# Attention scores as plain float32 matmuls on two halves of TensorE's rows, in place of a split into two fp32r parts

## The chip, the cores and the metric

One core of a Trainium2 chip runs the kernel. The metric is the device time of one execution in microseconds (us), median of several runs.

## The reference

Two stages. Attention with a learned relative position bias: batch 4, 8 heads, 576 positions, head dimension 64. Then a feed-forward stage with the maximum of three projections.

```
scores = q @ k.T / sqrt(64)                              # 4 x 8 x 576 x 576
x      = log1p(|i - j|) / log1p(max(i, 1))
bias   = relu(x * w1 + b1) @ w2                          # hidden 32, one bias per head
attn   = softmax(scores + bias);  attn /= sum(attn) + 1e-9
y      = attn @ v                                        # to 2304 x 512
h      = max(y @ w1m, y @ w2m, y @ w3m)                  # d_ff 768
out    = h @ w_out
```

Inputs of the attention are float32; the weights of the feed-forward stage are float64.

## The kernel before

**Bias stage.** 36 groups of 16 rows of the bias are computed (`hid` on VectorE and ScalarE, products `bp` on TensorE, scaled copies `bs`) and written to a DRAM tensor `bias_d` by DMA. SyncE (SP) issues all DMAs in program order. During this stage the first q and k are loaded and prepared (`prep(0)`, spread over groups 5 to 9), those of the second unit are loaded at group 16, and the first rows of the bias are read back (`load_bias`).

**Attention.** There are 16 units: 4 pairs of heads times 4 batches. For each unit `load_qk` brings q and k in twice, to partitions 0 to 63 and again to 64 to 127 (four DMAs). `prep` splits them: `qh` is q rounded to fp32r, `ql` the rest, `ks` holds k rounded on the lower partitions and its rest on the upper ones. It issues four casts and one subtraction on VectorE and three subtractions on GpSimd, one or two instructions after each of five steps. One matmul over 128 rows then gives q-part times (k high + k low), and two of them (`qh`, `ql`) make one half of a score tile.

A unit has 9 steps: for each of 4 tiles of 128 query rows one step for each of the two heads, and a last step for the 64 rows that are left of both heads (they stand together on 128 rows). In each engine the instructions run in program order, so the order in `step` is the schedule:

- `norm(n-2)`: VectorE adds 1e-9 and takes the reciprocal of the sums, GpSimd scales the exponentials `e` by it.
- `front(n)`: TensorE makes the scores of one head in `s` (two PSUM buffers), VectorE adds the bias and takes the minimum (`shift` below; a custom instruction and a read of its accumulator).
- `expo(n-1)`: ScalarE takes the exponential.
- `pvq`: up to two of the queued products of a group of query rows with v are run. A group has 5 entries in the queue: 4 pairs (each two matmuls of 64 output columns, one for each head, on the two halves of TensorE's columns) and one for the left-over keys (`vl`, all 128 columns), then a copy on ScalarE (`xhi`) and a subtraction on VectorE (`xlo`). The groups are 256 and 320 rows.
- `back(n-4)`: TensorE transposes `e` (four blocks into `tp`, and one or two into `lp`), ScalarE copies them to `et`; VectorE copies 1 to 3 of the 9.

A float32 matmul is recorded as two instructions (two passes), an fp32r one as one.

**Feed-forward stage.** It follows when the last `xhi` and `xlo` are there, and isn't touched by the change; the conversion of its first weights (`w0`) is done in small pieces between attention steps.

Of the kernel before, what the change touches and what calls it, by code (L numbers as in the profile page):

```python
# [19 lines left out]
def kernel(  # L20
# [12 lines left out]
    nc = tc.nc  # L33
# [131 lines left out]
    # attention, one pair of heads at a time  # L165
    units = [(hp, b) for hp in range(HP) for b in range(B)]
    order = [(t, h) for t in range(NTQ) for h in range(2)] + [(NTQ, 0)]
    NS = len(order)

    TS = 2  # L170
    sched = [(un, i) for un in range(len(units)) for i in range(NS)]
    NSTEP = len(sched)
    LAG = 4

    class Attention:
        def __init__(self, pool):
            self.pool = pool
            self.data = {}
            self.st = {}
            self.et = {}  # L180
            self.pvq = []
            self.preps = []
            self.vl = [pool.tile([128, 2 * D], F32, name=f"vl{x}", bufs=1) for x in range(2)]
            for x in self.vl:
                nc.gpsimd.memset(x, 0.0)
            bias_t.extend(pool.tile([128, 2, S], F32, name=f"bias{t}", bufs=1) for t in range(NTQ))
            bias_t.append(pool.tile([128, S], F32, name="biasm", bufs=1))

        def load_qk(self, un):
            pool, (hp, b) = self.pool, units[un]  # L190
            kr = pool.tile([128, 2 * S + 64], F32, tag="kr", bufs=1, name=f"kr{un}")
            qr = pool.tile([128, 2, S + 64], F32, tag="qr", bufs=1, name=f"qr{un}")
            hs = slice(2 * hp, 2 * hp + 2)
            for dst, src in ((kr, kd[b, hp]), (qr, qd[b, :, hs])):
                for x in (0, 64):
                    nc.sync.dma_start(out=dst[x:x + 64], in_=src)
            self.data[un] = dict(kr=kr, qr=qr)
# [12 lines left out]
        def prep(self, un):  # L210
            pool, u = self.pool, self.data[un]
            kr, qr = u.pop("kr"), u.pop("qr")
            ks = pool.tile([128, 2 * S + 64], F32R, tag="ks", bufs=2, name=f"ks{un}")
            qh = pool.tile([128, 2, S + 64], F32R, tag="qh", bufs=2, name=f"qh{un}")
            ql = pool.tile([128, 2, S + 64], F32R, tag="ql", bufs=2, name=f"ql{un}")
            u.update(ks=ks, qh=qh, ql=ql)
            p = slice(64, 128)
            kc = (slice(0, S), slice(S, 2 * S + 64))

            def sub_k(h):  # L220
                r = kc[h]
                nc.gpsimd.tensor_tensor(out=ks[p, r], in0=kr[p, r], in1=ks[p, r].bitcast(F32), op=ALU.subtract)  # L222

            def sub_q(h):
                nc.gpsimd.tensor_tensor(out=ql[:, h], in0=qr[:, h], in1=qh[:, h].bitcast(F32), op=ALU.subtract)

            nc.vector.tensor_copy(ks[:, kc[0]], kr[:, kc[0]])
            yield
            sub_k(0)
            nc.vector.tensor_copy(qh[:, 0], qr[:, 0])  # L230
            yield
            sub_q(0)
            nc.vector.tensor_copy(ks[:, kc[1]], kr[:, kc[1]])
            yield
            sub_k(1)
            nc.vector.tensor_copy(qh[:, 1], qr[:, 1])
            yield
            (nc.vector if un else nc.gpsimd).tensor_tensor(out=ql[:, 1], in0=qr[:, 1],
                                                           in1=qh[:, 1].bitcast(F32), op=ALU.subtract)
            yield  # L240

        def front(self, n):
            un, i = sched[n]
            t, h = order[i]
            pool, u = self.pool, self.data[un]
            s = ps_s(f"s{un}_{i}")
            ks, qh, ql = u["ks"], u["qh"], u["ql"]
            for x in range(2):
                r = slice(128 * t, 128 * t + 128)
                c0 = HALF * x  # L250
                ops = [(w, h, S * h + c0) for w in (qh, ql)]
                if t == NTQ:
                    ops += [(w, 1, S + LEFT + c0) for w in (qh, ql)]
                for j, (w, e, c) in enumerate(ops):
                    nc.tensor.matmul(s[:, x, 0:HALF], lhsT=w[:, e, r], rhs=ks[:, c:c + HALF],  # L255
                                     start=(j == 0), stop=(j == len(ops) - 1))
            sn = pool.tile([128, S], F32, tag="sn", bufs=2, name=f"sn{un}_{i}")
            nm = pool.tile([128, 1], F32, tag="nm", bufs=4, name=f"nm{un}_{i}")
            bt = bias_t[t][:, h] if t < NTQ else bias_t[t]
            nc.vector.tensor_tensor_reduce(  # L260
                out=sn.rearrange("p (a b) -> p a b", a=2), in0=s[:, :, 0:HALF],
                in1=bt.rearrange("p (a b) -> p a b", a=2), op0=ALU.add, op1=ALU.min,
                scale=-0.125, scalar=3e38, accum_out=nm)
            self.st[n] = (sn, nm)

        def expo(self, n):
            pool = self.pool
            sn, nm = self.st[n]
            h = order[sched[n][1]][1]
            if h == 0:  # L270
                self.e2 = pool.tile([128, 2 * S], F32, tag="e", bufs=3, name=f"e{n}")
            e = self.e2[:, S * h:S * h + S]
            sm = pool.tile([128, 1], F32, tag="sm", bufs=4, name=f"sm{n}")
            nc.scalar.activation(e, sn, ACTF.Exp, scale=-1.0, bias=nm, accum_out=sm)  # L274
            self.st[n] = (e, sm, self.e2)

        def norm(self, n):
            e, sm, e2 = self.st[n]
            rc = self.pool.tile([128, 1], F32, tag="rc", bufs=4, name=f"rc{n}")
            nc.vector.tensor_scalar(out=sm, in0=sm, scalar1=1e-9, scalar2=None, op0=ALU.add)  # L280
            nc.vector.reciprocal(rc, sm)  # L281
            nc.gpsimd.tensor_scalar(out=e, in0=e, scalar1=rc, scalar2=1.0, op0=ALU.mult, op1=ALU.mult)  # L282
            self.st[n] = (e, e2)

        def back(self, n):
            un, i = sched[n]
            t, h = order[i]
            pool, st = self.pool, self.st
            e, e2 = st.pop(n)
            ts = TS  # L290
            g = 0 if t < ts else 1
            w = 128 * ts if g == 0 else S - 128 * ts
            if i in (0, 2 * ts):
# [4 lines left out]
            c0 = 128 * t - 128 * ts * g  # L298
            tp = ps_t(f"tp{un}_{i}")
            for c in range(NTQ):  # L300
                k0 = 128 * c + LEFT * h
                nc.tensor.transpose(tp[:, 128 * c:128 * c + 128], e[:, k0:k0 + 128], ident)  # L302
            if t < NTQ:
                o, src = ea[:, :, h, c0:c0 + 128], tp.rearrange("p (c q) -> p c q", c=NTQ)
            else:
                o, src = ea[:, :, :, c0:c0 + LEFT], tp.rearrange("p (c h q) -> p c h q", c=NTQ, h=2)
            if i in ((4, 5, 6) if n < NSTEP - 102 else (5,)):
                nc.vector.tensor_copy(o, src)
            else:
                nc.scalar.copy(o, src)  # L310
            if t == NTQ or h == 1:
                lp = psum.tile([128, 128], F32, tag="l", bufs=1, name=f"lp{un}_{i}")
                m = 128 if t < NTQ else LEFT
                if t < NTQ:
                    nc.tensor.transpose(lp, e2[:, LB:S + LEFT], ident)
                else:
                    nc.tensor.transpose(lp, e[:, LB - 64:S], swap)
                    nc.tensor.transpose(lp[0:64], e[:, LB:S], ident)
                nc.scalar.copy(el[:, c0:c0 + m], lp[:, 0:m])
            if i == 2 * ts - 1 or i == NS - 1:  # L320
                self.queue_pv(un, 128 * ts * g, w, ea, el)
# [24 lines left out]
        def step(self, n, more=None):  # L346
            if 0 <= n - 2 < NSTEP:
                self.norm(n - 2)
            if n < NSTEP:
                un, i = sched[n]  # L350
                hp, b = units[un]
                nxt = un + 1
                if un < len(units) - 1:
                    if i == 0 and un:
                        self.load_qk(nxt)
                    if i == 8:
                        self.load_v(nxt)
                    if i == 3:
                        self.preps.append(self.prep(nxt))
                self.front(n)  # L360
                if b == B - 1 and hp + 1 < HP:
                    if i % 2 == 1 or i == NS - 1:
                        load_bias(hp + 1, i // 2)
            if more is not None:
                next(more, None)
            if 0 <= n - 1 < NSTEP:
                self.expo(n - 1)
            if len(self.pvq) == NTQ + 1 and self.wait:
                k, self.wait = 0, False
            else:  # L370
                k = 2 if len(self.pvq) >= 3 else 1
            if 0 <= n - LAG < NSTEP:
# [212 lines left out]
```

## Time and profile before

| | |
|---|---|
| median of 3 runs | 639.22 us (638.99 to 639.39) |
| profiled execution, span from the first instruction to the last | 637.4 us |
| bias stage, to the first `shift` | 0 to 61.2 us |
| attention, to the first matmul of the feed-forward stage | 61.2 to 338.2 us |
| feed-forward stage | 338.2 to 637.4 us |

Of the profiled execution only the span is recorded; the runs' median is 1.8 us above it, which is what lies around the span. Times in the rows below are us from the span's start, durations us; those in the groups of instructions are the total in us and the mean in ns. "[0.61 <-DVE nm L260]" is idle time of that engine ahead of the instruction, and what ended it. PE is TensorE's matmuls, PEld its weight loads, DVE VectorE, ACT ScalarE, POOL GpSimd, SP SyncE.

### The profile page before, as it was taken

What the parts mean: (1) busy time and instruction counts of PE and PEld (TensorE: products, weight loads), DVE (VectorE), ACT (ScalarE), POOL (GpSimd) and SP (SyncE); (2) the same over time, 40 slices, a digit from 0 to 9 for tenths busy, and PEclk for the clock granted to TensorE, in tenths of its full rate; (3) what the DMA queues carried; (4) which work ended last, traced back from release to release, by engine and by line L of the source; (5) the groups of instructions that cost most, each with busy time, mean ns of one, the idle gap of its engine ahead of it and who ended that gap; (6) DMA issues with size and microseconds to landing.
All of it is one profiled execution on the core that took longest, in us unless ns stands there. A gap on an engine that the chain in (4) does not pass through costs nothing.

```text
span 637.4 us, 11303 instructions
## 1 busy us (share of the span) xinstructions
PE 606.6 (95%) x3960; PEld 469.2 (74%) x3960; DVE 429.3 (67%) x1164; ACT 293.5 (46%) x747; POOL 199.0 (31%) x203
## 2 busy tenths in 40 slices
PE   7679899999998999989999999999999999999997
PEld 4224667767776777767777888888888888888886
DVE  7986989979997999889964564655655464123331
ACT  7668667767776877767781000000000001034443
POOL 1200777767775777777740000000000000000000
PEclk9998999999999999999999999999999999999999
DMA  8688643754467446763201122112212120001111
GB/s 214 191 256 288 172 118 92 208 142 99 100 195 191 98 100 167 187 143 92 63 2 34 34 66 67 58 42 67 67 34 82 51 67 0 1 34 67 67 66 67
DMA packets 48376, 65.12 MB, mean 102 GB/s; under 512 B 22464, under 2 KB 31936, under 8 KB 48320
## 3 DMA queue, kind: packets, MB, share of 16 engines
q1 hardware_dynamic: 48320, 64.40, 36.5%
q8 instruction: 32, 0.52, 0.4%
q14 instruction: 24, 0.20, 0.1%
HBM read 48.77 MB, written 15.61 MB: 101 GB/s over the span
## 4 chain that ended last, share of the span: by engine, by line
PE 58%; DVE 22%; DMA 6%; issue 4%; POOL 4%; ACT 3%; SPq 2%; DVEq 0%; POOLq 0%; ACTq 0%
PE h L464 8%; PE h L463 8%; PE h L462 8%; DVE sn L260 6%; PE g L464 4%; PE g L463 4%; PE g L462 4%; PE o L487 4%; PE o L488 4%; DMA qr<-in_qd_dram 4%; PE o L486 4%; PE pv L334 3%; PE tp L302 3%; DVE hid L106 3%; PE s L255 3%
## 5 line engine op out<-in xcount | busy, mean ns | idle before, releaser
L282 POOL TENSOR_SCALAR e<-e,rc 128x576 f32<-128x576 f32 x144 | 121.7, 848 | 116.8 <-DVE rc L281 82.4
L274 ACT ACTIVATE e<-sn,nm 128x576 f32<-128x576 f32 x144 | 113.1, 786 | 53.4 <-DVE nm L260 37.5
L469 ACT COPY m<-h 128x512 f32<-128x512 f32 (+1 forms) x30 | 16.4, 546 | 202.8 <-PE h L464 196.3
L255 PE MATMUL s<-ks,qh 128*128 128x288 f32 x320 | 101.4, 334 | 3.9 <-DVE nm L260 3.7
L302 PE MATMUL tp<-ident,e 128*128 128x128 f32 x576 | 90.2, 279 | 8.6 <-POOL e L282 8.2
L260 DVE CUSTOM_DVE_ANT_0 sn<-s,bias 128x576 f32<-128x576 f32 x128 | 96.1, 751 | 3.1 <-PE s L255 2.9
L302 PEld LDWEIGHTS tp<-ident,e 128*128 128x128 f32 x576 | 65.9, 140 | 42.9 <-POOL e L282 26.8
L255 PE MATMUL s<-ks,ql 128*128 128x288 f32 x320 | 89.0, 294 | 0.0
L462 PE MATMUL h<-xhi,wh 128*128 128x512 f32 (+1 forms) x240 | 88.6, 369 | 0.0
L463 PE MATMUL h<-xlo,wh 128*128 128x512 f32 (+1 forms) x240 | 88.3, 368 | 0.0
L464 PE MATMUL h<-xhi,wl 128*128 128x512 f32 (+1 forms) x240 | 88.3, 368 | 0.0
L310 ACT COPY et<-tp 128x512 f32<-128x512 f32 x119 | 70.0, 588 | 20.2 <-PE tp L302 19.9
L334 PE MATMUL pv<-et,vt 128*64 128x320 f32 (+1 forms) x512 | 76.0, 418 | 0.1
L255 PEld LDWEIGHTS s<-ks,qh 128*128 128x128 f32 x320 | 60.3, 188 | 6.8 <-DVE nm L260 6.0
L255 PEld LDWEIGHTS s<-ks,ql 128*128 128x128 f32 x320 | 60.6, 189 | 0.0
L127 PE MATMUL bp<-hid,w2s 128*32 128x79 f32 (+48 forms) x640 | 42.8, 404 | 12.0 <-DVE hid L106 7.2
L222 POOL TENSOR_TENSOR ks<-kr,ks 64x576 fp32r<-64x576 f32 (+1 forms) x32 | 49.2, 1536 | 14.7 <-DMA bias_d<-bs 11.1
L441 DVE TENSOR_TENSOR hl<-ht,hh 128x128 fp32r<-128x128 f32 x108 | 23.4, 287 | 44.9 <-ACT hh L440 44.9
L463 PEld LDWEIGHTS h<-xlo,wh 128*128 128x128 f32 x240 | 45.3, 189 | 7.6
L462 PEld LDWEIGHTS h<-xhi,wh 128*128 128x128 f32 x240 | 45.3, 189 | 7.6
L464 PEld LDWEIGHTS h<-xhi,wl 128*128 128x128 f32 x240 | 45.2, 188 | 7.5
L470 DVE TENSOR_TENSOR m<-h,m 128x512 f32<-128x512 f32 (+1 forms) x30 | 19.1, 637 | 46.8 <-ACT m L469 46.7
(77 smaller groups left out, 1032.5 us busy)
## 6 DMA issues: line engine op xcount, KB each, us to landing
bias_d<-bs SPq DMA_DIRECT2D x36, 295.5 KB, 4.3
qr<-in_qd_dram SPq DMA_DIRECT2D x32, 320.0 KB, 6.1
kr<-in_kd_dram SPq DMA_DIRECT2D x32, 304.0 KB, 4.5
bias<-bias_d SPq DMA_DIRECT2D x16, 576.0 KB, 4.0
w<-in_moe_w_dram SPq DMA_DIRECT2D x18, 512.0 KB, 3.5
out_dram<-ot SPq DMA_DIRECT2D x17, 256.0 KB, 2.0
vt<-in_v_dram SPq DMA_DIRECT2D x32, 128.0 KB, 2.4
w64o<-in_moe_w_out_dram SPq DMA_DIRECT2D x6, 512.0 KB, 3.6
```

Of the source, the lines that this page charges most:

```text
L127: nc.tensor.matmul(bp[32 * c:32 * c + 32, o:o + w], lhsT=w2s, rhs=src, start=True, stop=True)
L222: nc.gpsimd.tensor_tensor(out=ks[p, r], in0=kr[p, r], in1=ks[p, r].bitcast(F32), op=ALU.subtract)
L255: nc.tensor.matmul(s[:, x, 0:HALF], lhsT=w[:, e, r], rhs=ks[:, c:c + HALF], start=(j == 0), stop=(j == len(ops) - 1))
L260: nc.vector.tensor_tensor_reduce(out=sn.rearrange("p (a b) -> p a b", a=2), in0=s[:, :, 0:HALF], in1=bt.rearrange("p (a b) -> p a b", a=2) ...
L274: nc.scalar.activation(e, sn, ACTF.Exp, scale=-1.0, bias=nm, accum_out=sm)
L282: nc.gpsimd.tensor_scalar(out=e, in0=e, scalar1=rc, scalar2=1.0, op0=ALU.mult, op1=ALU.mult)
L302: nc.tensor.transpose(tp[:, 128 * c:128 * c + 128], e[:, k0:k0 + 128], ident)
L310: nc.scalar.copy(o, src)
L334: nc.tensor.matmul(pv[p], lhsT=u["vt"][:, c, h], rhs=ea[:, c, h], start=(c == 0), stop=False)
L462: nc.tensor.matmul(o, lhsT=hi[:, r], rhs=x, start=(c == 0), stop=False)
L463: nc.tensor.matmul(o, lhsT=hi[:, r], rhs=y, start=False, stop=False)
L464: nc.tensor.matmul(o, lhsT=lo[:, r], rhs=x, start=False, stop=(c == KDM - 1))
```

## The change

`prep` is gone, with its buffers. q and k stay float32 and are loaded once: head 0 of the pair on partitions 0 to 63, head 1 on 64 to 127, one DMA each (the host lays them out so). A step is now a tile of query rows of both heads, so a unit has 5 steps. Its scores are four float32 matmuls, two on the upper and two on the lower 64 rows of TensorE, each head into a PSUM buffer of its own; those of the left-over rows are two matmuls over all 128 rows, in which zeros in q keep the heads apart. The lag between `front` and the transposes goes from 4 steps of a head to 2 steps of a pair, sums are normalized for two heads at a time, VectorE always copies the transposes of head 1, and up to three entries of `pvq` run in a step, behind the transposes where they stood ahead of them.

```diff
-    LAG = 4
+    LAG = 2
         def load_qk(self, un):
-            kr = pool.tile([128, 2 * S + 64], F32, tag="kr", bufs=1, name=f"kr{un}")
-            qr = pool.tile([128, 2, S + 64], F32, tag="qr", bufs=1, name=f"qr{un}")
...
+            ks = pool.tile([128, S + LEFT], F32, tag="ks", bufs=2, name=f"ks{un}")
+            qs = pool.tile([128, S + LEFT], F32, tag="qs", bufs=2, name=f"qs{un}")
+            nc.sync.dma_start(out=qs, in_=qd[b, hp])
+            nc.sync.dma_start(out=ks, in_=kd[b, hp])
-        def prep(self, un):
...
         def front(self, n):
+            ss = [ps_s(f"s{un}_{t}_{h}") for h in range(nh)]
             for x in range(2):
+                for h in range(nh):
+                    if t < NTQ:
+                        p, r = slice(64 * h, 64 * h + 64), slice(128 * t, 128 * t + 128)
+                        c = LEFT * (1 - h) + HALF * x
+                    else:
+                        p, r, c = slice(0, 128), slice(LB, LB + 128), LEFT + HALF * x
+                    nc.tensor.matmul(ss[h][:, x, 0:HALF], lhsT=qs[p, r], rhs=ks[p, c:c + HALF],
+                                     start=True, stop=True)
...
         def step(self, n, more=None):
+            m, f = n - 1, n - LAG
...
+                    if t == 0 and un:
+                        self.load_qk(un + 1)
+                    if t == 4:
+                        self.load_v(un + 1)
+                nh = self.heads(n)
+                self.front(n)
+                self.shift(n, 0)
+            back = 0 <= f < NSTEP
+            if back:
+                tps, left = self.flip(f)
+                nc.scalar.copy(*tps[0])
+            if nh:
+                self.expo(n, 0)
+            if nh > 1:
+                self.shift(n, 1)
+            if n < NSTEP and b == B - 1 and hp + 1 < HP:
+                load_bias(hp + 1, t)
+            if 0 <= m < NSTEP:
+                self.norm(m)
+            if nh > 1:
+                self.expo(n, 1)
+            if back:
+                nc.scalar.copy(*left)
+                if len(tps) > 1:
+                    nc.vector.tensor_copy(*tps[1])
             if more is not None:
+                for _ in range(2):
+                    next(more, None)
+            k = 3 if len(self.pvq) >= 3 else 2
+            run, self.pvq = self.pvq[:k], self.pvq[k:]
+            for x in run:
+                x()
+            if back:
...
+                if t in (TS - 1, NS - 1):
+                    self.queue_pv(un, 128 * TS * g, w, *self.et)
@@ bias stage and attention loop
-                    first = at.prep(0)
-                if 5 <= g < 10:
-                    next(first)
-            at.step(n, w0 if n >= NSTEP - 102 and n % 3 == 0 else None)
+            at.step(n, w0 if n >= NSTEP - 57 and n % 3 == 0 else None)
```

`shift`, `norm` and `flip` hold the same instructions as `front`, `norm` and `back` did, for two heads at a time; `flip` issues the transposes of both heads and of `lp`.

## Rows read from the trace of the kernel before

**Rows 1.** The page of the profile: busy time by engine, and the chain of work that ended last by engine.

```profile
PE 606.6 (95%) x3960; PEld 469.2 (74%) x3960; DVE 429.3 (67%) x1164; ACT 293.5 (46%) x747; POOL 199.0 (31%) x203
...
PE 58%; DVE 22%; DMA 6%; issue 4%; POOL 4%; ACT 3%; SPq 2%; DVEq 0%; POOLq 0%; ACTq 0%
```

**Rows 2.** Busy time of each engine in the last two units (start:end, length, then busy time and number of instructions of each engine, granted clock, DMA share, GB/s).

```profile
297.85:314.92 17.07, 16.45 (x120) 12.43 (x118) 15.96 (x48) 12.90 (x33) 12.62 (x13) 1.00 0.45 107
314.92:329.59 14.67, 14.24 (x104) 11.25 (x105) 11.37 (x43) 11.89 (x31) 7.10 (x10) 1.00 0.06 21
```

**Rows 3.** Timeline of VectorE: the last `shift` of units 0, 3, 4 and 15.

```profile
74.44 0.76 DVE L260 CUSTOM_DVE_ANT_0 sn<-s,biasm 128x576 f32<-128x576 f32 x1
...
124.41 0.75 DVE L260 CUSTOM_DVE_ANT_0 sn<-s,biasm 128x576 f32<-128x576 f32 x1
...
143.36 0.76 DVE L260 CUSTOM_DVE_ANT_0 sn<-s,biasm 128x576 f32<-128x576 f32 x1
...
329.59 0.76 DVE L260 CUSTOM_DVE_ANT_0 sn<-s,biasm 128x576 f32<-128x576 f32 x1 [0.16 <-PE s L255]
```

**Rows 4.** Timeline of VectorE between the second and the third of these: a cast of `prep` that waits.

```profile
133.05 0.46 DVE L227 CAST ks<-kr 128x576 fp32r<-128x576 f32 x1 [1.60 <-DMA kr<-in_kd_dram]
```

**Rows 5.** Timeline of one and a half steps of unit 8: TensorE, its weight loads, and one row of VectorE.

```profile
200.36 0.60 PE L302 MATMUL tp<-ident,e 128*128 128x128 f32 x4
...
200.71 0.38 PE L255 MATMUL s<-ks,qh 128*128 128x288 f32 x1
...
200.93 0.30 PE L255 MATMUL s<-ks,ql 128*128 128x288 f32 x1
...
201.06 0.30 PE L255 MATMUL s<-ks,qh 128*128 128x288 f32 x1
...
201.20 0.29 PE L255 MATMUL s<-ks,ql 128*128 128x288 f32 x1
...
201.42 1.30 PE L334 MATMUL pv<-et,vt 128*64 128x320 f32 x8
...
202.65 0.66 PE L302 MATMUL tp<-ident,e 128*128 128x128 f32 x4
...
203.65 0.08 DVE L260 DVE_READ_ACCUMULATOR2_ANT nm<- 128x1 f32 x1
203.79 0.19 PEld L255 LDWEIGHTS s<-ks,qh 128*128 128x128 f32 x1 [0.61 <-DVE nm L260]
...
203.90 0.19 PEld L255 LDWEIGHTS s<-ks,ql 128*128 128x128 f32 x1
```

**Rows 6.** Timeline of TensorE: the left-over keys' matmul (two passes over 320 columns), behind a score matmul, and, in the end phase, behind a pair.

```profile
207.48 0.70 PE L331 MATMUL pv<-et,vl 128*128 128x320 f32 x2
...
337.81 0.81 PE L331 MATMUL pv<-et,vl 128*128 128x320 f32 x2
```

**Rows 7.** Groups of instructions on line 334: number of records, and their shortest, median and longest duration in ns.

```profile
L334 PE MATMUL pv<-et,vt x512: 379/432/484, 72.9 to 337.4; 128*64 128x256 f32 x86, 128*64 128x320 f32 x85
```

**Rows 8.** Groups of instructions on TensorE in the last unit, 314.92 to 329.59 us.

```profile
L334 PE MATMUL pv<-et,vt 128*64 128x320 f32 x16 | 2.6, 445 | 0.0
...
L334 PE MATMUL pv<-et,vt 128*64 128x256 f32 x8 | 1.1, 392 | 0.0
```

**Rows 9.** Timeline: a score's last matmul and the `shift` that waited for it; then VectorE's sequence of a `shift`, the two instructions of `norm` and the next `shift`.

```profile
324.76 0.29 PE L255 MATMUL s<-ks,ql 128*128 128x288 f32 x1
...
325.09 0.76 DVE L260 CUSTOM_DVE_ANT_0 sn<-s,bias 128x576 f32<-128x576 f32 x1 [0.46 <-PE s L255]
...
63.18 0.76 DVE L260 CUSTOM_DVE_ANT_0 sn<-s,bias 128x576 f32<-128x576 f32 x1
...
63.90 0.15 DVE L280 TENSOR_SCALAR sm<-sm 128x1 f32<-128x1 f32 x1
64.09 0.16 DVE L281 RECIPROCAL rc<-sm 128x1 f32<-128x1 f32 x1
64.17 0.74 DVE L260 CUSTOM_DVE_ANT_0 sn<-s,bias 128x576 f32<-128x576 f32 x1
```

**Rows 10.** Groups of instructions of the whole trace: GpSimd's scaling, ScalarE's exponential, VectorE's copy of a transpose.

```profile
L282 POOL TENSOR_SCALAR e<-e,rc 128x576 f32<-128x576 f32 x144 | 121.7, 848 | 116.8 <-DVE rc L281 82.4 <-ACT e L274 17.9 <-PE tp L302 5.9
L274 ACT ACTIVATE e<-sn,nm 128x576 f32<-128x576 f32 x144 | 113.1, 786 | 53.4 <-DVE nm L260 37.5 <-DVE sm L280 15.5
...
L308 DVE COPY et<-tp 128x512 f32<-128x512 f32 x25 | 17.1, 682 | 0.9 <-PE tp L302 0.9
```

**Rows 11.** Timeline of VectorE in the bias stage, around the casts of `prep(0)` (a row of several instructions runs from the first one's start to the last one's end).

```profile
12.52 0.46 DVE L227 CAST ks<-kr 128x576 fp32r<-128x576 f32 x1
12.88 2.39 DVE L106 TENSOR_SCALAR hid<-sm,bp 128x480 f32<-128x480 f32 x3
...
21.18 6.44 DVE L106 TENSOR_SCALAR hid<-sm,bp 128x432 f32<-128x432 f32 x15
```

**Rows 12.** Timeline of SP in the bias stage: the load of the second unit's q and k.

```profile
32.21 1.33 SPq L196 DMA_DIRECT2D kr<-in_kd_dram  x2
33.64 1.23 SPq L196 DMA_DIRECT2D qr<-in_qd_dram  x2
```

**Rows 13.** The chain of work that ended last, in order of time, at that place.

```profile
34.96 7.38 DMA bias_d<-bs
```

**Rows 14.** Timeline of SP: the read of the left-over rows' bias, after the bias stage.

```profile
70.61 0.48 SPq L161 DMA_DIRECT2D biasm<-bias_d  x1
```

More of the change, by code (lines that the diff above doesn't have):

```diff
@@ L166 @@
     units = [(hp, b) for hp in range(HP) for b in range(B)]
-    order = [(t, h) for t in range(NTQ) for h in range(2)] + [(NTQ, 0)]
-    NS = len(order)
+    NS = NTQ + 1
     TS = 2
-    sched = [(un, i) for un in range(len(units)) for i in range(NS)]
+    sched = [(un, t) for un in range(len(units)) for t in range(NS)]
     NSTEP = len(sched)
-    LAG = 4
+    LAG = 2
     class Attention:
@@ L208, in load_v, with heads, front @@
             self.data[un].update(vt=vt, vl=vl)
-        def prep(self, un):
+        def heads(self, n):
+            return 2 if sched[n][1] < NTQ else 1
+        def front(self, n):
+            un, t = sched[n]
             pool, u = self.pool, self.data[un]
[L212 to L247, printed above, removed]
-            for x in range(2):
[L249 to L258, printed above, removed]
+            nh = self.heads(n)
@@ L259, in front, with shift @@
+            self.st[n] = dict(s=ss)
+        def shift(self, n, h):
+            un, t = sched[n]
+            pool, st = self.pool, self.st[n]
+            sn = pool.tile([128, S], F32, tag="sn", bufs=3, name=f"sn{n}_{h}")
+            nm = pool.tile([128, 1], F32, tag="nm", bufs=4, name=f"nm{n}_{h}")
             bt = bias_t[t][:, h] if t < NTQ else bias_t[t]
             nc.vector.tensor_tensor_reduce(
-                out=sn.rearrange("p (a b) -> p a b", a=2), in0=s[:, :, 0:HALF],
+                out=sn.rearrange("p (a b) -> p a b", a=2), in0=st["s"][h][:, :, 0:HALF],
@@ L262, in front @@
                 in1=bt.rearrange("p (a b) -> p a b", a=2), op0=ALU.add, op1=ALU.min,
                 scale=-0.125, scalar=3e38, accum_out=nm)
[L264 to L269, printed above, removed]
-            if h == 0:
[L271 to L275, printed above, removed]
+            st[h] = (sn, nm)
@@ L279, in norm @@
-            rc = self.pool.tile([128, 1], F32, tag="rc", bufs=4, name=f"rc{n}")
+            st, nh = self.st[n], self.heads(n)
+            sm = st["sm"][:, 0:nh]
+            rc = self.pool.tile([128, 2], F32, tag="rc", bufs=3, name=f"rc{n}")
             nc.vector.tensor_scalar(out=sm, in0=sm, scalar1=1e-9, scalar2=None, op0=ALU.add)
-            nc.vector.reciprocal(rc, sm)
-            nc.gpsimd.tensor_scalar(out=e, in0=e, scalar1=rc, scalar2=1.0, op0=ALU.mult, op1=ALU.mult)
-            self.st[n] = (e, e2)
@@ L285, in back @@
[L285 to L293, printed above, removed]
+            nc.vector.reciprocal(rc[:, 0:nh], sm)
+            for h in range(nh):
+                e = st["e"][:, S * h:S * h + S]
+                nc.gpsimd.tensor_scalar(out=e, in0=e, scalar1=rc[:, h:h + 1], scalar2=1.0,
+                                        op0=ALU.mult, op1=ALU.mult)
@@ L297, in back @@
             ea, el = self.et
[L298 to L302, printed above, removed]
+            c0 = 128 * t - 128 * TS * g
+            tps = []
+            for h in range(self.heads(n)):
+                tp = ps_t(f"tp{un}_{t}_{h}")
+                for c in range(NTQ):
+                    k0 = S * h + 128 * c + LEFT * h
+                    nc.tensor.transpose(tp[:, 128 * c:128 * c + 128], e2[:, k0:k0 + 128], ident)
+                if t < NTQ:
+                    o, src = ea[:, :, h, c0:c0 + 128], tp.rearrange("p (c q) -> p c q", c=NTQ)
+                else:
+                    o, src = ea[:, :, :, c0:c0 + LEFT], tp.rearrange("p (c h q) -> p c h q", c=NTQ, h=2)
+                tps.append((o, src))
+            lp = psum.tile([128, 128], F32, tag="l", bufs=1, name=f"lp{un}_{t}")
+            m = 128 if t < NTQ else LEFT
             if t < NTQ:
-                o, src = ea[:, :, h, c0:c0 + 128], tp.rearrange("p (c q) -> p c q", c=NTQ)
+                nc.tensor.transpose(lp, e2[:, LB:S + LEFT], ident)
             else:
[L306 to L321, printed above, removed]
+                nc.tensor.transpose(lp, e2[:, LB - 64:S], swap)
+                nc.tensor.transpose(lp[0:64], e2[:, LB:S], ident)
+            return tps, (el[:, c0:c0 + m], lp[:, 0:m])
         def queue_pv(self, un, c0, w, ea, el):
@@ L346, in step @@
         def step(self, n, more=None):
-            if 0 <= n - 2 < NSTEP:
-                self.norm(n - 2)
+            m, f = n - 1, n - LAG
+            nh = 0
             if n < NSTEP:
-                un, i = sched[n]
+                un, t = sched[n]
                 hp, b = units[un]
[L352 to L359, printed above, removed]
-                self.front(n)
-                if b == B - 1 and hp + 1 < HP:
-                    if i % 2 == 1 or i == NS - 1:
-                        load_bias(hp + 1, i // 2)
@@ L364, in step @@
-            if more is not None:
[L365 to L372, printed above, removed]
-                run, self.pvq = self.pvq[:k], self.pvq[k:]
-                for f in run:
-                    f()
-                self.back(n - LAG)
-            if self.preps:
-                for _ in self.preps[0]:
-                    break
-                else:
-                    self.preps.pop(0)
+                if un + 1 < len(units):
+                    if t == 0 and un:
+                        self.load_qk(un + 1)
+                    if t == 4:
+                        self.load_v(un + 1)
```

47 lines of the change are left out of this document (32 added, 15 removed).

## Prediction, before the change was run

> **What bounds the kernel now.** I read the page first: TensorE is busy 95% of the span and leads the chain of waits with 58%, VectorE follows with 22% [rows 1]. A busy TensorE is not yet a full one, since its matmuls overlap, so I then went to the attention's timeline and counted starts. The reader should look at distances between starts, not at durations. Four score matmuls of 288 columns start 0.13 us apart though each lasts 0.29 [rows 5]. Transposes: four end 0.60 after the first start, the last one lasting 0.27, so they start 0.109 apart [rows 5]. The left-over keys' two float32 passes over 320 columns take 0.70 with an end of 0.43, so one pass holds the engine 0.27 [rows 6]; that is 2 cycles a column at the granted clock of 1.00, the upper level of 2.4 GHz [rows 2]. Eight passes of the pairs take 1.30 together [rows 5], one lasting 0.43 [rows 7]: one behind the other they would need 7 x 0.27 + 0.43 = 2.3. So the two halves of the columns run side by side, and a pair costs 0.54 at 320 columns and 0.43 at 256.
>
> TensorE changes its shape around each burst of pairs. Without a change the pairs' first load would start at 201.20 + 0.13 = 201.33; it starts at 201.42, and the first load (0.05) lies open: 0.145. Back, the last pass ends at 201.42 + 1.30 - 0.43 + 0.27 = 202.56, the transposes' first load comes at 202.65 and is open for 0.06: 0.15 [rows 5].
>
> A unit then needs of TensorE: 40 score matmuls x 0.131 = 5.24; 42 transposes x 0.109 = 4.58; pairs and left-overs 5 x 0.54 + 5 x 0.43 = 4.85; four bursts of pairs with 4 x (0.145 + 0.15) = 1.18. Sum 15.85. The last unit tests it: it has no `prep` beside it, and lacks 8 of 32 passes of the pairs [rows 8], one burst: 15.85 - 0.86 - 0.30 = 14.69, against 14.67 measured [rows 2]. So without `prep` the old order is bound by TensorE. With it a unit takes (329.59 - 74.44) / 15 = 17.01 on the average, and 143.36 - 124.41 = 18.95 where a pair of heads begins [rows 3]; there VectorE's cast waits for q and k that come behind the bias loads [rows 4], and everything behind it on VectorE waits too. What `prep` costs is thus about 1.2 us a unit, and this is the most that its removal can give there.
>
> **The change, part by part.** *What goes.* VectorE's busy time falls from 15.96 to about the 11.37 of the unit without `prep`, GpSimd's from 12.6 to 7.1 [rows 2]; both are then far from a bound. Four loads of a unit become two.
>
> *Scores.* Four float32 matmuls of two passes, each 0.27 x 288/320 = 0.242. With the heads side by side 4 x 0.242 = 0.97 for a tile of both, against 8 x 0.131 = 1.05; the left-over tile 2 x 2 x 0.242 = 0.97. A unit: 4.84 in place of 5.24. No row shows matmuls on halves of the rows; the nearest, on halves of the columns, run fully side by side [rows 5, 7], and one behind the other would be 1.94. I take 0.97 and keep 1.94.
>
> TensorE also hides each load behind the pass before it in the same rows: 0.131 a matmul leaves no room for a 128-column load, of which 0.11 shows where it is open (203.79 to 203.90) [rows 5]. The Trainium skill (TensorE: Matmul & The Clock Gate, part 3, The mechanism) says that a load overlaps running matmuls only when its row group differs; by that three more loads of 0.11 would be open in each tile, 1.3 us a unit; these rows contradict it for the plain mode.
>
> *Changes of shape.* The new order is scores on row halves, transposes on the full array, pairs on column halves. Into row halves: 0.09 and an open load of 0.11 (as 203.79 to 203.90 [rows 5]), 0.20; four a unit, 0.79. From there to the transposes 0.15 x 4 = 0.60. Into the pairs 0.145 x 4 = 0.58. From pairs to `vl`, now in one step, 0.20 x 2 = 0.39 (0.81 for the two passes there against 0.70 shows the open load [rows 6]). Together 2.36, against 1.18. That row halves are changed into at the price of column halves is an estimate; the bounds are 0 and twice it. TensorE's need: 4.84 + 4.58 + 4.85 + 2.36 = 16.63, 0.8 more than before.
>
> *A new wait.* One step now takes both score buffers, so `front(n+1)` waits for both `shift`s of step n. From the first load: 0.11 + 0.97 to the last column; `shift` starts 0.33 behind the start of a 0.13 matmul [rows 9], so 0.20 behind the last column: at 1.28. The second follows 0.74 later, at 2.02, and lasts 0.76 (63.18 and 63.90 [rows 9]); a load that waited for one started 0.06 behind the read of its accumulator (203.73 to 203.79 [rows 5]): 2.85. A step with pairs holds TensorE 3.4 us or more and hides this. But a unit's ten queue entries run as 3 and 2, 3 and 2, so that one step in five (t = 1) has none; it has 0.11 + 0.97, 0.15, six transposes 0.65, done at 1.9. The next scores: head 0's first half runs while TensorE waits; the other three start at 2.85 and end at 2.85 + 0.11 + 0.97 = 3.93, where without the wait it would be 1.9 + 0.09 + 0.11 + 0.97 = 3.07. Lost: 0.86. `norm` of the step before stands on VectorE behind both `shift`s, at 2.74, and takes 0.35 (63.90, 64.09 and 0.16 [rows 9]); GpSimd scales two heads at 0.85 each [rows 10], until 4.8; the transposes of head 1 would start at 3.93 + 0.15 + 0.44 = 4.52: 0.28 more. The copy and subtraction of the product before lie ahead of the first `shift` on VectorE, behind two exponentials of 0.79 [rows 10] on ScalarE; I estimate 0.15. Sum 1.29, bounds 0.8 and 2. A unit: 16.63 + 1.29 = 17.92, 0.91 more than before; 15 units: +13.6.
>
> The other edits are hidden. `load_bias` of a tile is issued behind both its `shift`s and has five steps until it is read; what stands behind it on SP (`load_v`, `load_qk`) is needed a unit later. On the engines: VectorE has, for a tile, two `shift`s, `norm`, and a copy of 0.68 [rows 10], 0.74 x 2 + 0.35 + 0.68 = 2.5 of 3.4. The conversions of `w0` come two at a time from step 23 on; where they meet the step without pairs they delay it: +1 (0 to 3).
>
> *First unit and end.* From the first `shift` to the last one of unit 0 it is now 74.44 - 61.2 = 13.2; three waits of 2.9 and one of 2.3 make 11.1, but the left-over rows' bias is only asked for at 70.61, 9.4 behind the first `shift` [rows 14], and lands later: I take 12, -1. The end phase stays at 338.2 - 329.6 = 8.6: the transposes of two tiles and the last group's five entries stand behind the last `shift` in either order.
>
> *Bias stage.* Three `hid` take 2.39 while GpSimd's subtractions run beside them, against 6.44 for 15 later [rows 11]: 0.8 against 0.43 each. With three such groups, 3.3, and four casts of some 0.4, VectorE loses 4.6 there. Loading the second unit holds SP 2.6 [rows 12] right ahead of a write of the bias that takes 7.38 on the chain [rows 13]; half of both kinds goes. I take 6 of it (3 to 8.5), since the writes fill the DMA engines behind it.
>
> Sum: 637.4 + 13.6 + 1 - 1 - 6 = 645 for the span, and the 1.8 by which the runs' median lies above it: 647.
>
> **The rivals.** *Changes of shape are cheap on row halves.* The eight that touch them cost 1.39 a unit in my sum. At nothing it is 647 - 15.5 x 1.39 = 625: faster (15.5 units, as the first and the last take part in it by half). It decides at 7.8 / 15.5 = 0.5 us a unit, that is where one costs below 0.11 instead of 0.17. For it: no row shows one. Against: both kinds that are shown, into and out of column halves, cost 0.145 and more.
>
> *Row halves don't run side by side*, so the change does half of what it says. Each tile costs 0.97 more; at t = 1 the wait eats nearly nothing of it: 3.8 us a unit, 15.5 x 3.8 = 59: 706. Against it: pairs on column halves do run so.
>
> *They overlap in part.* With a quarter of the overlap lost a tile costs 0.97 + 0.97/4 = 1.21, four times a unit: 15.5 x 0.97 = 15: 662. The rows speak for full overlap. The Trainium skill (TensorE: Matmul & The Clock Gate, part 3, measured speedups) gives a measured speedup of 3.07 for four tiles of 32 rows, about three quarters; no run here shows it.
>
> **How the numbers follow.** My forecast, about 641 to 655: 0.48. Cheap changes (625 to 638): 0.25. Gain and loss cancel: 0.08. Overlap in part (655 to 675): 0.09. None (around 706): 0.10. Measurements of this kernel can tell a difference of 0.2%, 1.3 us, from none. So faster 0.25, same 0.08, slower 0.67. The range 627 to 668 leaves out the last case and the ends of two others.
>
> **What would show it.** Right: score passes of the two heads starting together and four matmuls within about 1.1 us; gaps of some 0.1 us at the score's both ends; in the step without pairs TensorE waiting for `nm`; a unit of 17.9; the first `shift` at 55. Wrong: a unit below 17.0, or transposes following scores without a gap; passes 0.24 apart in single file mean the second rival.

## The result, and the profile after

The new kernel takes 645.05 us (median of 8 runs, 644.36 to 647.74) against 639.36 for the old one (8 runs): a ratio of 1.008, 95% interval 1.0055 to 1.0105. The new kernel is slower by some 6 us, 0.8%; forecast were 647.

The page of the new kernel, its lines of busy time and of the chain by engine:

```profile
PE 631.3 (98%) x3896; PEld 446.1 (69%) x3896; DVE 374.2 (58%) x996; ACT 270.3 (42%) x708; POOL 110.6 (17%) x154
...
PE 85%; POOL 4%; ACT 4%; DVE 3%; DMA 2%; issue 2%; DVEq 0%; POOLq 0%; ACTq 0%
```

VectorE fell from 22% of the chain to 3%, GpSimd's busy time by 88 us, and TensorE took their place in the chain [rows 1]. The work that is gone lay on engines that had room; TensorE, which had none, got more changes of shape and a new wait, as the rows below show.

Timeline of TensorE over one unit of the new kernel, from the scores of t = 1 to those of the next t = 1:

```profile
199.71 1.24 PE L223 MATMUL s<-ks,qs 64*128 64x288 f32 x8
200.88 0.66 PE L275 MATMUL tp<-ident,e 128*128 128x128 f32 x4
201.37 0.27 PE L286 MATMUL lp<-swap,e 128*128 128x128 f32 x1
201.48 0.27 PE L287 MATMUL lp<-ident,e 128*64 128x128 f32 x1
201.80 1.91 PE L223 MATMUL s<-ks,qs 64*128 64x288 f32 x8
203.77 1.38 PE L275 MATMUL tp<-ident,e 128*128 128x128 f32 x8
204.98 0.27 PE L284 MATMUL lp<-ident,e 128*128 128x128 f32 x1
205.18 1.83 PE L301 MATMUL pv<-et,vt 128*64 128x320 f32 x12
206.95 1.24 PE L223 MATMUL s<-ks,qs 64*128 64x288 f32 x8
208.12 1.09 PE L275 MATMUL tp<-ident,e 128*128 128x128 f32 x8
...
217.59 1.24 PE L223 MATMUL s<-ks,qs 64*128 64x288 f32 x8
```

and the median duration of one of those score passes (line 223 from 90 to 320 us: shortest, median and longest in ns):

```profile
L223 PE MATMUL s<-ks,qs x460: 402/403/507, 91.6 to 319.7; 64*128 64x288 f32 x128, 128*128 128x288 f32 x26
```

Eight passes take 1.24 us, though each lasts 0.40 and holds its rows for 0.242: one after the other they would need 7 x 0.242 + 0.40 = 2.1. The two heads do run side by side. From the first score pass of the tile at 206.95 to the first transpose at 208.12 it is 1.17, which is the 0.11 + 0.97 + 0.09 of the forecast. The scores at 201.80 are those behind the step without products: 1.91 in place of 1.24, and the eight transposes behind them take 1.38 in place of 1.09. What they wait for is seen in the timeline of the weight loads:

```profile
201.80 0.29 PEld L223 LDWEIGHTS s<-ks,qs 64*128 64x128 f32 x2 [0.31 <-DVE nm L233]
202.48 0.78 PEld L223 LDWEIGHTS s<-ks,qs 64*128 64x128 f32 x6 [0.38 <-DVE nm L233]
203.76 0.42 PEld L275 LDWEIGHTS tp<-ident,e 128*128 128x128 f32 x4 [0.51 <-POOL e L256]
204.48 0.42 PEld L275 LDWEIGHTS tp<-ident,e 128*128 128x128 f32 x4 [0.30 <-POOL e L256]
```

Head 0 waits for its `shift` until 201.80, head 1 for the second one until 202.48, and the transposes of head 1 wait for GpSimd's scaling until 204.48.

The last `shift` of units 0, 1, 14 and 15 on VectorE, to be held against [rows 3], and the windows of the last two units, against [rows 2]:

```profile
66.85 0.75 DVE L233 CUSTOM_DVE_ANT_0 sn<-s,biasm 128x576 f32<-128x576 f32 x1
...
85.81 0.75 DVE L233 CUSTOM_DVE_ANT_0 sn<-s,biasm 128x576 f32<-128x576 f32 x1
...
320.25 0.75 DVE L233 CUSTOM_DVE_ANT_0 sn<-s,biasm 128x576 f32<-128x576 f32 x1
...
338.13 0.75 DVE L233 CUSTOM_DVE_ANT_0 sn<-s,biasm 128x576 f32<-128x576 f32 x1
```

```profile
302.37:320.25 17.88, 17.71 (x116) 10.86 (x115) 13.39 (x38) 11.09 (x30) 7.46 (x9) 1.00 0.19 54
320.25:338.13 17.88, 17.72 (x116) 10.86 (x115) 10.97 (x36) 11.08 (x30) 6.60 (x9) 1.00 0.15 40
```

Most units take 17.88, where the old ones took 14.7 (the last) and otherwise 16.1 to 19.0. A few take 18.0 to 18.9, where pieces of the weights' conversion fall, two take 17.7, and the first interval takes 18.96 (the last section says why).

The bias stage, on VectorE: the first 42 `hid` run without a break, to 20.6 us, where the old kernel had casts and slowed `hid` between them [rows 11], and the first `shift` comes at 54.17 where it came at 61.2.

```profile
4.75 15.88 DVE L106 TENSOR_SCALAR hid<-sm,bp 128x576 f32<-128x576 f32 x42
...
54.17 0.76 DVE L233 CUSTOM_DVE_ANT_0 sn<-s,bias 128x576 f32<-128x576 f32 x1 [2.05 <-PE s L223]
```

The two spans then differ as follows: bias stage -7.0; from there to the last `shift` of unit 0 12.7 against 13.3, -0.6; fifteen units 271.3 against 255.15, +16.1; the end phase 8.6 in both; the feed-forward stage 299.2 in both. Sum +8.5, and 646.0 - 637.4 = 8.6. The profiled run took 647.74 in all, 2.7 above the runs' median; the last section says where. Some 2 of the +16.1 come from the same stretch at a lower clock.

### The profile page after: what moved, and what is told of

The parts are those of the page before. It is cut to its first block, busy times and chain, and to the rows that moved or that the text cites. A ratio compares the mean times of both kernels' runs of the same rounds, so it can differ in the third digit from the quotient of the medians.

```text
span 646.0 us, 10696 instructions
## 1 busy us (share of the span) xinstructions
PE 631.3 (98%) x3896; PEld 446.1 (69%) x3896; DVE 374.2 (58%) x996; ACT 270.3 (42%) x708; POOL 110.6 (17%) x154
## 4 chain that ended last, share of the span: by engine, by line
PE 85%; POOL 4%; ACT 4%; DVE 3%; DMA 2%; issue 2%; DVEq 0%; POOLq 0%; ACTq 0%
PE s L223 11%; PE pv L301 11%; PE tp L275 10%; PE h L441 8%; PE h L440 8%; PE h L439 8%; POOL e L256 4%; PE g L441 4%; PE g L440 4%; PE g L439 4%; PE o L464 4%; PE o L465 4%; PE o L463 4%; PE pv L298 3%; PE bp L127 3%; ACT e L245 2%
## 5 line engine op out<-in xcount | busy, mean ns | idle before, releaser
L256 POOL TENSOR_SCALAR e<-e,rc 128x576 f32<-128x576 f32 x144 | 109.2, 770 | 230.4 <-ACT e L245 128.9
L233 DVE CUSTOM_DVE_ANT_0 sn<-s,bias 128x576 f32<-128x576 f32 x128 | 91.9, 755 | 66.8 <-PE s L223 66.7
L223 PE MATMUL s<-ks,qs 64*128 64x288 f32 (+1 forms) x576 | 111.8, 437 | 1.9 <-DVE nm L233 1.0
L223 PEld LDWEIGHTS s<-ks,qs 64*128 64x128 f32 (+1 forms) x576 | 62.2, 189 | 43.0 <-issue 17.2
L330 ACT COPY et<-tp 128x512 f32<-128x512 f32 x80 | 46.8, 585 | 107.7 <-PE tp L275 107.6
L275 PEld LDWEIGHTS tp<-ident,e 128*128 128x128 f32 x576 | 63.3, 142 | 36.8 <-POOL e L256 18.3
L275 PE MATMUL tp<-ident,e 128*128 128x128 f32 x576 | 84.1, 283 | 4.0 <-POOL e L256 2.5
L301 PEld LDWEIGHTS pv<-et,vt 128*64 128x64 f32 x512 | 31.1, 136 | 24.2 <-issue 7.9
L344 DVE COPY et<-tp 128x512 f32<-128x512 f32 x64 | 43.3, 676 | 3.7 <-PE tp L275 2.5
L439 PE MATMUL g<-xhi,wh 128*128 128x512 f32 (+1 forms) x120 | 44.1, 368 | 0.0
```

The lines of the kernel that those rows point to most:

```text
L223: nc.tensor.matmul(ss[h][:, x, 0:HALF], lhsT=qs[p, r], rhs=ks[p, c:c + HALF], start=True, stop=True)
L233: nc.vector.tensor_tensor_reduce(out=sn.rearrange("p (a b) -> p a b", a=2), in0=st["s"][h][:, :, 0:HALF], in1=bt.rearrange("p (a b) -> p a ...
L256: nc.gpsimd.tensor_scalar(out=e, in0=e, scalar1=rc[:, h:h + 1], scalar2=1.0, op0=ALU.mult, op1=ALU.mult)
L275: nc.tensor.transpose(tp[:, 128 * c:128 * c + 128], e2[:, k0:k0 + 128], ident)
L301: nc.tensor.matmul(pv[p], lhsT=u["vt"][:, c, h], rhs=ea[:, c, h], start=(c == 0), stop=False)
L330: nc.scalar.copy(*tps[0])
```

## The experiments

Eight kernels, each timed beside the old one on the same chip. The old one had medians of 640.09 there for the first four and 640.75 for the others.

**1. Products spread over the steps.**

```diff
-            k = 3 if len(self.pvq) >= 3 else 2
+            k = (1, 2, 3, 2, 2)[n % NS]
```

> The new order, with 1, 2, 3, 2, 2 entries of the product queue in the steps t = 0 to 4 of a unit in place of 2, 0, 3, 2, 3; nothing else differs. Theory (TensorE is the bound in every step but the one without products, where it waits for both shifts): that wait goes, one more change of shape of 0.145 us comes; a unit takes 16.8 to 17.1 us in place of 17.88, the whole 645.05 - 15 x 0.8 to 1.1 = 629 to 633 us. Rival (each step pays for holding both score buffers, wherever the products run): a unit of 17.7 to 18, the whole 643 to 646.

Measured: 633.23 us, 0.990 of the old kernel (0.987 to 0.993). Units take 16.84 where no conversion falls. Timeline of TensorE in its step t = 1 (from 206.31) and the start of the next:

```profile
206.31 1.24 PE L223 MATMUL s<-ks,qs 64*128 64x288 f32 x8
207.48 0.66 PE L275 MATMUL tp<-ident,e 128*128 128x128 f32 x4
...
208.29 0.65 PE L301 MATMUL pv<-et,vt 128*64 128x256 f32 x4
208.87 0.70 PE L298 MATMUL pv<-et,vl 128*128 128x256 f32 x2
209.50 1.24 PE L223 MATMUL s<-ks,qs 64*128 64x288 f32 x8
```

The scores at 209.50 are back to 1.24, and 1.04 us of the unit is gone. Holding both score buffers in a step costs only where TensorE has nothing else to do; the rival falls. TensorE's need was worked out as 16.63 + 0.145 = 16.77, so next to nothing but that need is left.

**2. Scores on all rows.**

```diff
-                        p, r = slice(64 * h, 64 * h + 64), slice(128 * t, 128 * t + 128)
+                        p, r = slice(0, 128), slice(128 * t, 128 * t + 128)
```

> The new order, but each score matmul takes all 128 rows, so the scores of both heads are added together and the softmax is that of the sum: the same number of matmuls and columns, no halves of rows. Theory (the halves run side by side, and a change into or out of them costs 0.15 to 0.2 us): the four matmuls of a tile take 4 x 0.485 = 1.94 us in place of 0.97, eight changes of shape of 1.39 us in all go, a unit is 16.63 - 1.39 + 3.88 = 19.1 plus a wait of some 0.3, 19.4; the whole 645 + 15.5 x 1.5 = 668. Rival (changes of shape to row halves cost nothing, something else fills the 17.88): a unit of about 20.9, the whole 690 or more.

Measured: 674.43 us, a unit of 19.81. Its timeline of TensorE around a tile's scores:

```profile
207.45 2.21 PE L223 MATMUL s<-ks,qs 128*128 128x288 f32 x8
209.50 1.04 PE L275 MATMUL tp<-ident,e 128*128 128x128 f32 x8
...
211.15 0.70 PE L298 MATMUL pv<-et,vl 128*128 128x256 f32 x2
211.69 2.10 PE L223 MATMUL s<-ks,qs 128*128 128x288 f32 x8
```

A tile takes 2.1 or 2.2, as eight passes in single file do, and transposes and the left-over keys' product join it without a gap (eight transposes take 1.04 where they took 1.09 behind row halves). The expectation was 6 us short: it took all eight changes of shape away, but two of the four tiles still stand behind pairs on column halves, and their scores still pay 0.2 to get out of that shape (the 2.21 against 2.10 is its open load). With 0.4 more a unit, 19.4 becomes 19.8. The rival's 20.9 is out; side by side and with its changes of shape, the row halves' version is 1.9 us a unit faster than this.

**3. The old kernel with one preparation.**

```diff
-                    if i == 3:
-                        self.preps.append(self.prep(nxt))
...
-            ks, qh, ql = u["ks"], u["qh"], u["ql"]
+            u0 = self.data[0]
+            ks, qh, ql = u0["ks"], u0["qh"], u0["ql"]
```

> The old kernel, but only the first unit's q and k are split, and all later units use that split: fifteen times four casts and four subtractions are left out, the loads stay. Theory (the old order without prep is bound by TensorE at 15.85 us a unit): 17.0 - 15.85 to 16.0 = 1.0 to 1.15 a unit less, the whole 639.3 - 15 to 17 = 622 to 624. Rival (prep only filled idle time of VectorE and GpSimd, and what the new kernel loses is not bought with anything): 636 to 639.

Measured: 625.29 us, 0.977 of the old kernel (0.975 to 0.979), a little short of the expected. Windows of its two last units:

```profile
283.78:299.83 16.05, 16.05 (x121) 12.43 (x119) 12.12 (x43) 12.72 (x34) 6.71 (x10) 1.00 0.43 99
299.83:315.83 16.00, 16.00 (x120) 12.37 (x118) 11.50 (x42) 12.65 (x34) 6.69 (x9) 1.00 0.15 44
```

TensorE is busy through all of them: 16.0 against the 15.85 counted. So `prep` costs the old kernel 1.0 us a unit on the average, 14.8 us in all (255.15 - 240.4), and the old order of TensorE without it is 1.85 us a unit below the new one's 17.88. The cost isn't spread evenly. The last `shift` of units 3 and 4, to be held against 124.41 and 143.36 in [rows 3]:

```profile
123.31 0.76 DVE L261 CUSTOM_DVE_ANT_0 sn<-s,biasm 128x576 f32<-128x576 f32 x1 [0.16 <-PE s L256]
...
139.26 0.76 DVE L261 CUSTOM_DVE_ANT_0 sn<-s,biasm 128x576 f32<-128x576 f32 x1 [0.16 <-DMA vl<-in_v_dram]
```

It is 15.95 here and was 18.95. The three units that begin a new pair of heads give 8.8 of the 14.8 us, 2.9 each, the other twelve 0.5 each. In those three `prep` also waited for its loads [rows 4]; what share is the wait and what the work, this experiment doesn't tell apart.

**4 and 5. What shortened the bias stage.** Into the new kernel's bias stage went back either the casts and subtractions of the first `prep`, on tiles that nobody reads, or the second half of the loads.

```diff
+        nc.vector.tensor_copy(a[:, 0:S], ks[:, 0:S])
+        yield
+        nc.gpsimd.tensor_tensor(out=c[p, 0:S], in0=ks[p, 0:S], in1=a[p, 0:S].bitcast(F32), op=ALU.subtract)
...
```

> The new kernel, with the casts and subtractions of the first prep put back into the bias stage at their old places, into tiles that nobody reads; the loads stay halved. Theory (the bias stage got 7 us shorter mostly because VectorE no longer runs these and no longer shares with GpSimd): the first shift comes 4 to 5 us later than 54.2, and the whole is 648 to 650. Rival (the halved loads did it): the first shift within 1.5 us of 54.2, the whole 645 to 646.5.

```diff
                     at.load_qk(0)
+                    twice(bp, 0)
...
                     at.load_qk(1)
+                    twice(bp, 1)
```

> The new kernel, with the q and k of the first two units loaded once more in the bias stage, into tiles that nobody reads, so that SP issues and the DMA engines move there what they did before. Theory (after the ballast on VectorE moved the first shift by 5.9 us, some 1 us of the 7.0 is left for the loads): first shift at 54.5 to 56, the whole 645 to 647. Rival (the two overlap: either alone brings most of it back): first shift at 57 or later, the whole 648 or more.

Measured: 652.77 us with the casts and subtractions, 647.78 with the loads. The kernel with casts and subtractions, on VectorE (the second row is one of the three `hid` of the first, by itself):

```profile
12.36 2.38 DVE L106 TENSOR_SCALAR hid<-sm,bp 128x480 f32<-128x480 f32 x3
...
12.74 1.63 DVE L106 TENSOR_SCALAR hid<-sm,bp 128x480 f32<-128x480 f32 x1
...
60.06 0.76 DVE L233 CUSTOM_DVE_ANT_0 sn<-s,bias 128x576 f32<-128x576 f32 x1 [2.55 <-PE s L223]
```

its first subtraction on GpSimd:

```profile
12.58 1.51 POOL L483 TENSOR_TENSOR bc<-ks,ba 64x576 fp32r<-64x576 f32 x1 [10.53 <-DVE ba L481]
```

and the kernel with the loads, on VectorE:

```profile
54.96 0.76 DVE L233 CUSTOM_DVE_ANT_0 sn<-s,bias 128x576 f32<-128x576 f32 x1 [1.99 <-PE s L223]
```

The first `shift` moves by 5.9 and by 0.8; together 6.7 of the 7.0. The traces of experiments 1, 2, 6, 7 and 8, whose bias stage is the new kernel's, have it at 53.3 to 54.7, so 0.8 is hardly more than such traces differ by, and 5.9 is far more. It was the preparation, more than the 4 to 5 us expected, and nearly not the loads.

Three `hid` beside a subtraction take 2.38 again, as in [rows 11], but they aren't slowed alike. The one that starts during the subtraction (12.58 to 14.09) lasts 1.63, until 0.28 behind its end; the next one takes 0.46, as `hid` without a neighbour on GpSimd do. So each of the four subtractions holds up one `hid`, by 1.2 to 1.3 us, and the four casts take some 0.4 each: 6.7 us together, of which 5.9 are left at the first `shift`.

The medians lie 7.7 and 2.7 above 645.05, and both wholes above what was expected (648 to 650, 645 to 647). Held against the old kernel timed beside each, the new kernel lies 5.7 above it, experiment 4 12.7 and experiment 5 7.0: 7.0 and 1.3 for the two changes, the second within the intervals.

**6 and 7. Products ahead of the transposes.** Once in the new kernel, once in that of experiment 1:

```diff
+            run, self.pvq = self.pvq[:k], self.pvq[k:]
+            posts = [y for y in [x() for x in run] if y]
             back = 0 <= f < NSTEP
             if back:
                 tps, left = self.flip(f)
...
-            run, self.pvq = self.pvq[:k], self.pvq[k:]
-            for x in run:
+            for x in posts:
                 x()
```

> The new kernel, with the queued products run between the scores and the transposes, as the old order had them; their copy and subtraction stay at the step's end. Theory (TensorE's need counts: one change of shape less in the steps t = 0 and 3, one more in t = 4, and GpSimd has time to scale head 1 before its transposes in t = 2): 0.15 + 0.28 us less a unit, 17.4 to 17.5; the whole 638 to 640. Rival (the later transposes hold back ScalarE's copies, which stand ahead of the exponentials, and so the next scaling): a unit of 17.9 or more, the whole 645 or more.

> Both: products as 1, 2, 3, 2, 2 and ahead of the transposes. Theory: the wait of the step without products is gone already, so only the change of shape is left to win, 0.15 us a unit: a unit of 16.7, the whole 630 to 632, against 633.2. Rival (the gains add up in full, 0.43): 626 to 627.

Measured: 682.44 and 679.73 us, both far slower; units of 20.27 and 20.15. The end of a group and the start of the next in experiment 6, on TensorE and ScalarE:

```profile
204.40 0.81 PE L298 MATMUL pv<-et,vl 128*128 128x320 f32 x2
...
207.84 0.43 ACT L307 CAST xhi<-pv 128x320 fp32r<-128x320 f32 x1
...
208.85 1.52 PE L301 MATMUL pv<-et,vt 128*64 128x256 f32 x12 [1.68 <-DVE xlo L308]
...
218.07 1.91 PE L223 MATMUL s<-ks,qs 64*128 64x288 f32 x8 [0.96 <-DVE nm L233]
```

the same end of a group in the new kernel:

```profile
192.06 0.81 PE L298 MATMUL pv<-et,vl 128*128 128x320 f32 x2
...
193.09 0.43 ACT L305 CAST xhi<-pv 128x320 fp32r<-128x320 f32 x1
...
194.75 1.52 PE L301 MATMUL pv<-et,vt 128*64 128x256 f32 x12
```

and TensorE in experiment 7:

```profile
210.96 1.08 PE L301 MATMUL pv<-et,vt 128*64 128x256 f32 x8 [1.69 <-DVE xlo L308]
...
221.91 1.83 PE L301 MATMUL pv<-et,vt 128*64 128x320 f32 x12 [1.64 <-DVE xlo L308]
```

There is one PSUM buffer for the products. In t = 4 the next group's first pair stands behind the scores and waits for `xlo` of the group before, which waits for ScalarE's copy `xhi`: TensorE stands still for 1.68. In both orders one step's transposes and one step's scores lie on TensorE between `vl` and that pair. What differs is when ScalarE copies: 1.03 behind the start of `vl` in the new kernel, 3.44 here, since the copy stands behind the transposes' copies and both exponentials on ScalarE, and the transposes now come behind the products.

In experiment 7 the second group, too, begins in the step after the end of the first, and the wait comes twice a unit: 1.69 + 1.64 = 3.3, which is its whole loss (20.15 against the 16.84 of experiment 1). In experiment 6 the loss is 20.27 - 17.88 = 2.4. The rest beside the 1.68 is mostly in the scores behind the step without products: they start 1.24 behind the start of the last transpose (216.83 to 218.07), in place of 0.32 in the new kernel (201.48 to 201.80), and the transposes behind them give 0.3 of it back (1.09 in place of 1.38).

The rival's bounds hold, and that later transposes hold ScalarE back is what it said; but both theory and rival had looked past the single buffer, which hands this on to TensorE. Counting TensorE's need tells the time only while nothing that it waits for is moved.

**8. Spread products, and conversions one at a time.**

```diff
-                for _ in range(2):
-                    next(more, None)
+                next(more, None)
...
-            at.step(n, w0 if n >= NSTEP - 57 and n % 3 == 0 else None)
+            at.step(n, w0 if n >= NSTEP - 38 else None)
```

> Products as 1, 2, 3, 2, 2, and the conversion of the first weights in single pieces, one in each of the last 40 steps, in place of two in every third step from step 23 on. Theory (VectorE has room for one piece in a step, and two of them are what makes some units 17.1 to 18.2 in place of 16.84): all units within 0.2 of 16.84, the whole 630 to 632. Rival (the long units are waits for DMAs, of the bias or of weights): no change, 633 to 634.

Measured: 631.77 us, 0.987 of the old kernel (0.983 to 0.990). The first eight intervals after the first are 16.84 flat, where experiment 1 had 18.17, 17.08 and 17.44 among them; the six behind them, where nearly all the pieces now fall, lie between 16.84 and 17.42. So pieces on VectorE do make the long units, and single ones still seem to do so a little. Against experiment 1 the gain is within the two intervals.

## Why the prediction was right

**What bounds the old kernel** held: without `prep` TensorE alone sets the pace (experiment 3: 16.0 to 16.05 for the 15.85 counted), and `prep` costs 1.0 a unit (1.2 was said). The forecast's own test of the 15.85, on the last unit of the old kernel, was no proof, though. Two more of TensorE's rows in that window, beside those of [rows 8]:

```profile
L255 PE MATMUL s<-ks,qh 128*128 128x288 f32 x18 | 5.7, 332 | 0.0
L302 PE MATMUL tp<-ident,e 128*128 128x128 f32 x34 | 5.4, 279 | 0.7 <-POOL e L282 0.7
```

It holds 36 score matmuls (18 with `qh` and as many with `ql`), not 40, and two transposes fewer than 42 (six more are those of `lp`), so the count for it is 14.69 - 0.52 - 0.22 = 13.95; the 14.67 measured had 0.7 of waiting for GpSimd in it. That 14.69 met 14.67 was luck; experiment 3 is what shows the bound.

**Scores.** The value taken, 0.97 for a tile of both heads, was right: the upper bound of 1.94 is what experiment 2 shows for single file, and the eight passes in 1.24 show side by side. The rivals of no overlap and of part of it are both out. The Trainium skill lists a speedup of 3.07 for four tiles of 32 rows (TensorE: Matmul & The Clock Gate, part 3, Measured speedup vs the span model); no run here has four tiles, and the two of 64 rows here lose nothing. Nor do further loads lie open within a tile: 0.11 + 0.97 + 0.09 leaves no room for them. The Trainium skill says that a load overlaps running matmuls only when its row group differs (the same page, part 3, The mechanism); in this trace each load of a tile but the first is hidden behind a pass on its own rows, so the trace disagrees.

**Changes of shape.** Taken at the price of column halves, 0.15 to 0.20, and so it came out: 1.17 from a tile's first score pass to the first transpose, and a unit of 16.84 in experiment 1 for a counted 16.77. The rival with cheap changes needed about 16.5 for the plain new kernel.

**The new wait.** Said was 1.29 a unit, of it 0.86 for the scores, 0.28 for GpSimd and 0.15 on VectorE. In the timeline the scores behind the step without products start 0.12 late (201.48 + 0.11 + 0.09 = 201.68 against 201.80), it is 1.97 from them to the first transpose in place of 1.17, and the transposes last 0.29 longer: 0.12 + 0.80 + 0.29 = 1.2. So the scores lose 0.92 and GpSimd's part is 0.29; the 0.15 doesn't show. Experiment 1 takes the wait away and gains 1.04, to which the added change of shape of 0.145 belongs: 1.19.

**Sums.** A unit 17.92 said, 17.88 measured, 0.6 less over fifteen units. The conversions of `w0` cost some 2 us and not 1 (the longer and the shorter units against 17.88). The first unit -0.6 and not -1, the end phase unchanged as said. The bias stage gave 7.0 and not 6. The split between VectorE and DMA was off: experiments 4 and 5 give 5.9 and 0.8 where 4.6 and up to 3.9 had been worked out. VectorE's term was too small because it counted three slowed groups of `hid`, 3.3 together, where there are four, 5.1 together (and 3.3 with four casts of 0.4 make 4.9, not 4.6).

For the profiled run the forecast is close: 645 said for the span, 646.0 measured. The single terms miss by up to 1 us in both directions and nearly cancel, so a part of this closeness is luck; and 1.1 of the measured, the first interval of 18.96 against 17.88, wasn't in the sum. The runs' median lies 2.7 below the profiled run, which lies 1 above the forecast: that is the 2 us by which 647 is too high, and no term of the sum explains it.

So the change does what it says, and removes 7 us in the bias stage and 15 us of preparation; it then pays more on TensorE. The scores themselves became cheaper there (4.84 in place of 5.24 a unit), but the new order has fourteen changes of shape in a unit in place of eight, 1.2 us more, and the step of two heads brings a wait of 1.2: 2.0 a unit by the count, 1.85 by the units measured (17.88 against 16.03 in experiment 3). Fifteen units take 271.3 against 240.4 in experiment 3, 30.9 more: 27.8 by these 1.85, 2 by the conversions, 1.1 by the first interval. Against that stand 14.8 for the preparation, 7.0 in the bias stage and 0.6 in the first unit, and 8.5 are left, as the spans have it.

## What to carry to other kernels

Count what the fullest engine holds, start to start, unit by unit, before taking work off another one: a change that frees engines with room can be paid for in changes of shape and waits on the one that has none, and busy time (95% before, 98% after) hardly shows them. When a step becomes larger, look for the step that has nothing to cover the new wait, and spread the queued work so that none is empty: here one line of run counts turns +0.8% into -1.0%, and of the kernels that compute the whole reference the one of experiment 8 has the lowest median, with that of experiment 1 within the noise. An order may also be covering for a single buffer; ask of each piece of work what waits behind it before moving it.

## What had not been expected

TensorE's granted clock falls to its lower level of 1.2 GHz for a stretch or more in nine of the ten traces; experiment 8's has none before the program ends. The profiled run of the new kernel has two, one in the bias stage and one behind it, seen in windows of 2 us (columns as in [rows 2]):

```profile
38.00:40.00 2.00, 0.00 (x0) 0.00 (x0) 2.00 (x7) 0.54 (x1) 0.00 (x0) 1.00 1.06 408
...
42.00:44.00 2.00, 2.00 (x20) 0.86 (x16) 1.28 (x3) 1.35 (x3) 0.00 (x0) 0.50 0.95 333
...
54.00:56.00 2.00, 1.61 (x8) 0.73 (x7) 1.45 (x4) 1.03 (x3) 0.00 (x0) 1.00 0.60 199
56.00:58.00 2.00, 1.61 (x10) 0.70 (x6) 1.52 (x5) 1.32 (x4) 0.00 (x0) 0.96 0.48 65
58.00:60.00 2.00, 2.00 (x7) 1.14 (x6) 0.82 (x2) 0.90 (x4) 1.46 (x2) 0.50 0.95 344
```

Ahead of the first, TensorE ran no matmul for 2 us. Ahead of the second lie the first steps of attention, in which it ran 8 and 10 matmuls in 2 us, where the windows from 46 to 54 have 27 to 49. In experiment 5 it ran 7 and 8 at the same place and the clock stayed at its upper level, so what decides it isn't shown.

With the second stretch the first interval between units took 18.96, and 18.97 in experiment 4, which has one behind its first `shift` too; in experiment 5, which has none there, it took 16.88. This is most of the 2.7 us by which the profiled run lies above the median. The runs go with it: the five of the new kernel with a mean granted clock of 0.997 took 644.36 to 645.15, the three with 0.991 or 0.995 took 646.49 to 647.74.
